# One fused attention and MoE kernel: the list of the first part in another order, and one table of engines

## The chip, the cores and the metric

One core of a Trainium2 chip runs the whole program. The metric is the device time of one execution in microseconds (us); a measurement is the median of several runs. The engines are TensorE (PE: matrix products into PSUM), VectorE (DVE), ScalarE (ACT), GpSimd (POOL) and SyncE (SP, which issues all DMAs). Each runs its own queue of instructions in order, and they wait for one another by semaphores.

## The reference

```python
def _attn_ref(q, k, v):                       # 4 batches, 8 heads, 576 positions, 64 wide
    q_d = q.reshape(B, H, Sd, 4, D).mean(axis=3)          # so do k_d and v_d; Sd = 144
    out_up = np.repeat(sm_attn(q_d, k_d, v_d), 4, axis=2)
    mask = np.abs(pos[:, None] - pos[None, :]) < 4
    scores = np.where(mask, scale * np.matmul(q, k.transpose(0, 1, 3, 2)), -1e9)
    return out_up + softmax(scores) @ v

x = attention, as 2304 tokens by 512
h = x @ w_in                                  # 512 x 2048
x = (h * (1 / (1 + np.exp(-1.702 * h)))) @ w_out           # 2048 x 512
h = x @ moe2_w_in
x = np.maximum(0.01 * h, h) @ moe2_w_out
```

## The kernel before, in words

The program has three parts that overlap. Attention works on 16 jobs, a batch and a pair of heads each, pair 0 to pair 15; four pairs make a batch and with it four rows of 128 features (kc 0 to 3) of the transposed x. The first MoE layer works on five blocks of tokens (512, 512, 512, 384, 384) by 16 slices of 128 hidden features; one such unit is 12 products for the first matrix (line 860) and 12 for the second (line 901). The second MoE layer comes last, from about 490 us.

All products are made with high parts and low parts: a number is cut into its rounded value (hi) and the rest (lo), and three products are added. So each weight tile and each block of x passes over several engines before TensorE can use it.

Up to unit 13 and attention pair 7 the order of the work is a list written out by hand, ORDER (line 52); `token` (line 1215) runs it word by word. A word is a step, a dot and a number; the part behind an @ chooses the engine (V, G or A) through `on` or `copy`, where the step asks one of these. Every engine gets its instructions in the order of this list. The words that matter here:

- `q.j`, `k.j`, `va.j`, `vb.j`, `vh.j`: loads of pair j, issued by SP. `w.n`: load of weight half n (n = 2m for the first and 2m+1 for the second matrix of slice m) into one of three buffers.
- `wF.n` (ACT, line 187), `wL.n` (DVE, 188), `wB.n` (DVE, 192): the float64 bits of a weight become float32, in one of three buffers t. `wH.n` (ACT, 159) and `wO.n` (POOL, or DVE with @V, 211): its high and low part; `wO` frees the buffer t.
- `Qd.j`, `Kd.j`: sums of four neighbours of q and k (`pool4`, line 427). It calls `nc.vector.tensor_reduce`.
- `Sd.j`, `Mxd.j`, `Exd.j`, `Rcd.j`, `Mud.j`: the attention over the sums: scores (PE, 549), row maxima (DVE, 556 and 560), exp (ACT, 566), one over the total (DVE, 519 and 520), divide (POOL, 530 and 532, or 539 from pair 4 on).
- `S0.j`, `S1.j`: local scores of one head of pairs 0 to 3 (PE, 449 and 455), into bank acc0 or acc1. `M0`, `M1` (DVE, 501) take the row maxima, `N0`, `N1` (DVE, 505) negate them, `E0`, `E1` (ACT, 510) take exp of the bank, and only then is the bank free for the next pair. `Rc.j` (519, 520) and `Mu.j` (POOL, 482) divide. Pairs 4 to 7 use `S.j` (PE, 455), `A0`, `A1` (DVE, 469), `Mx` (489), `Sb` (POOL, 482), `Ex` (ACT, 498), `Sm`, `Rc`, `Mu`.
- `T0`, `T1` (PE, 579) with `C0`, `C1` (ACT, 159) and `U0`, `U1` (PE, 651) with `D0`, `D1` transpose; `Vd.j` (PE, 632) with `Od.j` (ACT), and `Y0`, `Y1` (PE, 684) with `X0`, `X1` (DVE, 734) make the outputs, the rows of x.
- `xh.kc` (ACT, 159), `xl.kc` (843): high and low part of row kc of the first block; `h0.kc`, `h1.kc`: what units 0 and 1 make of it. `L.u`, `M.u`: the two halves of unit u; `Gt`, `Gd`, `Gh`, `Gl`: the gate between them (ACT 879, DVE 880, ACT 159, POOL or DVE 886).
- `z3.n`: n idle products in bank acc3 (line 1225), whose result nobody reads.

Behind the list a loop goes over the other units. At the end of each block it makes the high and low parts of the next one with `split_hi` and `split_lo` (line 840): there the tables XLO and (V, G, V, G) name the engine for each kc.

```python
def pool4(self, dst, src):                                       # line 426
    nc.vector.tensor_reduce(
        out=dst, in_=src.rearrange("p (g r) -> p g r", r=FACTOR), axis=AX.X, op=ALU.add
    )
XLO = [G, G, V, G]                                               # line 48
on(XLO[kc] if j < 3 else (V, G, V, G)[kc]).tensor_tensor(...)    # line 843
```

Of the kernel before, what the change touches and what calls it, by code (L numbers as in the profile page):

```python
# [7 lines left out]
F32 = mybir.dt.float32  # L8
# [5 lines left out]
ALU = mybir.AluOpType  # L14
# [13 lines left out]
def attn_moe_kernel(ctx: ExitStack, tc, qT_d, kT_d, vh_d, vg_d, w1a, w2a, w1b, w2b, outT):  # L28
# [3 lines left out]
    S = NT // B  # L32
# [14 lines left out]
    V, G = nc.vector, nc.gpsimd  # L47
    XLO = [G, G, V, G]
# [1 line left out]
    HEAD = 2  # L50
    LEAD = 3.0
    ORDER = """
        w.2 wF.2 wL.2 k.0 Kd.0 wB.2 wH.2 q.0 Qd.0 z3.14 S0.0 M0.0 S1.0 M1.0 va.4 Va0.4 Va1.4 w.0 wF.0 Sd.0 Mxd.0 Exd.0
        wO.2 wL.0 N0.0 E0.0 N1.0 Rcd.0 Mud.0 wB.0 wH.0 wO.0 k.1 q.1 z3.16 S0.1 Qd.1 Kd.1 M0.1 w.3 wF.3 wL.3 q.2 Sd.1
        Mxd.1 E1.0 Rc.0 Exd.1 vb.4 Vb0.4 wB.3 wH.3 wO.3 Vb1.4 Mu.0 Rcd.1 Mud.1 N0.1 E0.1 T0.0 C0.0 T1.0 C1.0 q.4 k.4
        z3.1 S.4 A1.4 k.2 va.1 w.1 wF.1 S1.1 M1.1 A0.4 Qd.2 Kd.2 Mx.4 Sb.4 z3.4 S0.2 M0.2 w.5 vb.7 wF.5 Qd.4 Sd.2 Mxd.2
        Exd.2 U0.0 D0.0 wL.5 N1.1 Kd.4 T0.1 k.3 z3.6 Sd.4 Rcd.2 Mud.2 wL.1 E1.1 Mxd.4 Exd.4 T1.1 C1.1 q.3 N0.2 E0.2 wB.5
        wH.5 wB.1 vb.2 Rc.1 Mu.1 Rcd.4 Mud.4 q.5 vb.0 k.5 z3.5 S.5 Qd.5 A1.5 Qd.3 A0.5 Kd.3 z3.6 U1.1 D1.1 S1.2 T0.2
        Kd.5 w.7 M1.2 wH.1 C0.1 wO.5 Vb0.7 U1.0 D1.0 wO.1 Mx.5 Sb.5 N1.2 Sd.3 S0.3 M0.3 Mxd.3 T1.4 wF.7 wL.7 va.0 T1.2
        w.4 wF.4 wL.4 w.6 wF.6 N0.3 wB.7 wB.4 E1.2 Rc.2 Mu.2 Ex.5 Exd.3 Rcd.3 Mud.3 C0.2 T0.4 C0.4 z3.4 S1.3 Vd.0 M1.3  # L60
        vh.0 Y0.0 k.6 va.6 va.5 vb.1 vh.4 C1.2 Od.0 X0.0 U0.1 D0.1 E0.3 wH.7 wO.7 C1.4 Ex.4 Y1.0 vh.1 va.2 vh.2 w.12
        vb.3 Vd.1 Od.1 w.9 X1.0 xh.0 wL.6 xl.0 N1.3 E1.3 Sm.5 wB.6 Sm.4 Rc.4 Mu.4 Rc.5 Sd.5 Mxd.5 T0.3 C0.3 Vd.4 Od.4
        wF.9 wH.4 wO.4 va.3 q.6 Vd.2 Y1.1 X1.1 h0.0 h1.0 U0.2 D0.2 T1.3 w.14 vh.3 Kd.6 Va0.5 Va1.5 Exd.5 Rc.3 C1.3 Y0.1
        U1.2 D1.2 X0.1 Qd.6 U1.4 D1.4 wL.9 Od.2 wH.6 xh.1 Y1.2 Y0.2 X1.2 Mu.3 U1.3 D1.3 U0.3 D0.3 X0.2 wF.12 xh.2 wB.9
        U0.4 D0.4 xl.1@V wO.6 xl.2 Y1.4 Vd.3 wH.9 wO.9 Od.3 Y0.3 X0.3 Y1.3 X1.3 xh.3 h0.1 wL.12 xl.3@V wF.14 wL.14 wB.12
        L.2 Gt.2 Gd.2 wH.12 wO.12@V Gh.2 Gl.2@V vb.5 Vb0.5 Rcd.5 Mud.5 w.8 wF.8 wL.8 h1.1 h1.2 h1.3 Gt.1 Gd.1 Gh.1 wB.14
        wB.8 wH.8 Gl.1@V Mu.5@V L.3 wO.8 h0.2 h0.3 Y0.4 Gt.0 Gd.0 Gh.0 X0.4 w.19 wF.19 w.15 wH.14 X1.4 Gl.0@V wL.19
        Vb1.5 L.6 wF.15 Va0.6 wL.15 wB.19 Gt.3 wO.14@V wB.15 T0.5 T1.5 C0.5 w.10 wF.10 wL.10 wH.19 wO.19 M.0 M.1 C1.5
        Vd.5 Gd.3 Gh.3 Gl.3 wB.10 wH.10 wO.10 Va1.6 Sd.6 Mxd.6 M.2 L.4 Od.5@V va.7 w.16 Gt.6 Gd.6 wF.16 wL.16 Exd.6 w.11
        wF.11 Rcd.6 Gh.6 wL.11 wB.11 wH.11 wB.16 wH.15 Gl.6@V wO.15 S.6 A0.6 A1.6 Mx.6 Mud.6 Sb.6 wO.11@V Gt.4 Gd.4  # L70
        wH.16 wO.16@V w.22 Gh.4 Gl.4@V wF.22 wL.22 vh.5 w.13 wF.13 wL.13 vb.6 w.20 wF.20 wL.20 M.3 U1.5 D1.5 U0.5 D0.5
        wB.13 wH.13 wO.13 L.5 Gt.5 wB.20 wH.20 Gd.5 Gh.5 Gl.5 Ex.6 wB.22 wH.22 wO.22 L.7 q.7 Qd.7 k.7 Kd.7 S.7 A1.7
        wO.20 Sm.6 Gt.7 Gd.7 M.4 w.18 wF.18 wL.18 wB.18 Gh.7 Gl.7@V wH.18 wO.18 Rc.6 A0.7 Mx.7 Sb.7 w.17 wF.17 wL.17 L.8
        Gt.8 Gd.8 M.5 M.6 Y0.5 t.22 w.24 X0.5 Gh.8 Gl.8@V Vb0.6 w.26 wF.26 wL.26 wB.26 Y1.5 L.9 Gt.9 wH.26 T1.6 C1.6
        w.28 wB.17 Gd.9 Gh.9 L.10 X1.5 Sd.7 Ex.7 wO.26 Mu.6@V wH.17 Gl.9@V wO.17 M.7 M.8 Sm.7 Gt.10 Gd.10 Rc.7 wF.24
        wL.24 wF.28 wL.28 wB.24 w.21 wF.21 wL.21 Mxd.7 wB.21 wB.28 wH.24 Gh.10 Gl.10@V Vb1.6 U0.6 D0.6 Exd.7 Rcd.7 Va0.7
        wH.28 L.11 Gt.11 Gd.11 T0.6 C0.6 U1.6 D1.6 Gh.11 wO.24 Mu.7@V Mud.7 wO.28@V M.9 w.23 wF.23 wL.23 wH.21 Vd.6 Od.6
        vh.6 Y1.6 w.25 wF.25 w.27 X1.6 Va1.7 Gl.11@V wB.23 wO.21@V Vb1.7 wL.25 wB.25 wF.27 wL.27 wH.23@V wO.23 L.12
        Gt.12 Gd.12 T0.7 C0.7 T1.7 L.13 t.25 wH.25 wO.25@V C1.7 w.29 w.31 Y0.6 X0.6 U0.7 D0.7 Gh.12 wF.29 wL.29 M.10
        U1.7 D1.7 Vd.7 Od.7 wB.27 wH.27 wO.27 Gl.12@V Gt.13 wF.31 Gd.13 Gh.13 Gl.13 wB.29 vh.7 Y0.7 X0.7 w.30 wF.30 Y1.7  # L80
        X1.7 wL.31 M.11 wL.30 wB.31 wH.31 wH.29 wO.29 wB.30 wH.30 wO.30 wO.31 t.27
    """
    MASKED = range(4)
    EARLY = 12
# [20 lines left out]
    def slot(name):  # L105
# [20 lines left out]
        out=ident, in_=ident, compare_op=ALU.not_equal, fill=1.0, base=0,  # L126
# [5 lines left out]
    for r in (slice(0, KT), slice(KT, P)):  # L132
        nc.gpsimd.affine_select(
            out=bands[r], in_=bands[r], compare_op=ALU.is_ge, fill=NEG, base=0,
# [3 lines left out]
            out=bands[r], in_=bands[r], compare_op=ALU.is_ge, fill=NEG, base=2 * HALO,  # L138
# [15 lines left out]
    def on(default):  # L154
        return chosen[0] or default
# [684 lines left out]
    def split_lo(j, kc):  # L840
        hi, lo = xs[kc]
        f = xf.pop((j, kc))[:, : blk[j][1]]
        on(XLO[kc] if j < 3 else (V, G, V, G)[kc]).tensor_tensor(out=lo, in0=f, in1=hi.bitcast(F32), op=ALU.subtract)  # L843

    gs = {}
    hs = {}
# [67 lines left out]
    class Second:  # L914

        B11, B12, B21, B22, T1, T2, T4 = range(7)
# [335 lines left out]
    with tc.manual_schedule(engines={ET.PE, ET.DVE, ET.Pool, ET.Activation, ET.SP}):  # L1252
# [4 lines left out]
        for kc in range(KC):  # L1257
            steps[f"xh.{kc}"] = lambda kc=kc: split_hi(0, kc)
            steps[f"xl.{kc}"] = lambda kc=kc: split_lo(0, kc)
            for m in range(HEAD):  # L1260
                steps[f"h{m}.{kc}"] = lambda kc=kc, m=m: l1_part(units[m], [kc], f"acc{m}")
# [23 lines left out]
        for u in range(UNITS, len(units)):  # L1285
            j, m = units[u]
            l1_part(units[u], range(KC))
            if m == NM - 1:
                for kc in range(KC):
                    if j + 1 < len(blk):  # L1290
                        split_hi(j + 1, kc)
                        split_lo(j + 1, kc)
# [85 lines left out]
```

## Time and profile before

| | |
|---|---|
| median of 3 runs | 851.44 us (850.66 to 851.85) |
| profiled execution | 849.98 us |
| its span | 848.2 us |
| TensorE busy | 837.6 us, 99% |
| VectorE busy | 538.5 us, 63% |
| ScalarE busy | 405.4 us, 48% |
| GpSimd busy | 474.8 us, 56% |
| chain that ended last | TensorE 94%, VectorE 2%, ScalarE, GpSimd, DMA and issue 1% each |

Times in the rows are from the start of the span. A busy share is a mean over stages that have different limits, so the stretches and the timeline are read beside it. "Idle before, releaser" at the end of a row is how long the engine had stood still, and what let it go on.

### The profile page before, as it was taken

Reading aid. Unit: us, or ns where it says so; the run is one execution under the profiler, and the core shown is the slowest. Engines: PE = TensorE matmul, PEld = TensorE weight load, DVE = VectorE, ACT = ScalarE, POOL = GpSimd, SP = SyncE. Lnnn points to the kernel's source line nnn. Section 1 sums busy time; section 2 is a strip of 40 time slices with the busy share of each in tenths; the row PEclk is TensorE's granted clock in tenths of the full one; section 3 lists DMA queues with packets and bytes.
Section 4 is the critical chain, followed back from the end, with each engine's and each line's share of the span. In section 5 each row is a group of like instructions: output and inputs, shape, how many; then the busy total and the mean of one; then the engine's idle time right before and its main releaser. Section 6 shows DMA issues by size and latency. Waiting matters only on the chain.

```text
span 848.2 us, 15692 instructions
## 1 busy us (share of the span) xinstructions
PE 837.6 (99%) x5736; PEld 761.2 (90%) x5736; DVE 538.5 (63%) x950; ACT 405.4 (48%) x972; POOL 474.8 (56%) x470
## 2 busy tenths in 40 slices
PE   8899999999999999999999999999999999999998
PEld 5677878887877888899999999999999999999997
DVE  6877776755567644567665756567564667573565
ACT  6866554433334334465555534445435464344460
POOL 6544433744446444776655823468555577454574
PEclk9999999999999999999999999999999999999999
DMA  8756545376664833999949978967779877887655
GB/s 298 248 157 183 187 145 151 111 231 180 191 198 148 243 119 123 349 346 415 364 157 338 336 252 274 345 229 275 253 263 360 275 243 261 278 290 260 217 195 177
DMA packets 76877, 204.95 MB, mean 242 GB/s; under 512 B 14656, under 2 KB 30016, under 8 KB 70400
## 3 DMA queue, kind: packets, MB, share of 16 engines
q1 hardware_dynamic: 76800, 203.95, 71.5%
q8 instruction: 45, 0.74, 0.4%
q14 instruction: 32, 0.26, 0.1%
HBM read 155.42 MB, written 48.50 MB: 240 GB/s over the span
## 4 chain that ended last, share of the span: by engine, by line
PE 94%; DVE 2%; ACT 1%; POOL 1%; DMA 1%; issue 1%; SPq 0%; POOLq 0%; ACTq 0%; DVEq 0%
PE h L860 23%; PE acc L901 23%; PE p L1107 21%; PE h L1032 21%; PE sc L455 2%; PE avd L632 1%; PE scd L549 1%; PE av L684 1%; DMA a<-qT 1%; PE av L700 0%; PE pt L651 0%; ACT a L566 0%; PE pdt L579 0%; DMA kT<-kT 0%; POOL xl L843 0%
## 5 line engine op out<-in xcount | busy, mean ns | idle before, releaser
L1086 POOL TENSOR_TENSOR ring<-raw,ring 128x384 fp32r<-128x384 f32 x148 | 166.6, 1137 | 144.6 <-ACT ring L1084 143.2
L860 PE MATMUL h<-xh,w 128*128 128x512 f32 (+1 forms) x640 | 197.6, 371 | 0.0
L1107 PE MATMUL p<-ring,v 128*128 128x384 f32 x900 | 178.8, 334 | 0.0
L901 PE MATMUL acc<-gh,w 128*128 128x512 f32 (+1 forms) x560 | 173.5, 372 | 0.0
L1107 PEld LDWEIGHTS p<-ring,v 128*128 128x128 f32 x900 | 158.0, 188 | 0.1
L1032 PE MATMUL h<-x,v 128*128 128x384 f32 x672 | 137.3, 334 | 0.0
L860 PEld LDWEIGHTS h<-xh,w 128*128 128x128 f32 x640 | 118.7, 188 | 16.8 <-issue 1.2
L886 POOL TENSOR_TENSOR gl<-g,gh 128x512 fp32r<-128x512 f32 (+1 forms) x59 | 72.2, 1224 | 96.8 <-ACT gh L159 96.2
L1032 PEld LDWEIGHTS h<-x,v 128*128 128x128 f32 x672 | 118.3, 188 | 0.0
L860 PE MATMUL h<-xl,w 128*128 128x512 f32 (+1 forms) x320 | 117.8, 368 | 0.4 <-POOL xl L843 0.4
L901 PEld LDWEIGHTS acc<-gh,w 128*128 128x128 f32 x560 | 104.0, 188 | 15.1 <-issue 0.6
L901 PE MATMUL acc<-gl,w 128*128 128x512 f32 (+1 forms) x280 | 103.7, 370 | 0.0
L880 DVE SCALAR_TENSOR_TENSOR g<-g,h 128x512 f32<-128x512 f32 (+1 forms) x80 | 50.4, 630 | 76.5 <-ACT g L879 76.2
L879 ACT ACTIVATE g<-h 128x512 f32<-128x512 f32 (+1 forms) x80 | 43.9, 549 | 98.5 <-PE h L860 96.6
L1039 ACT ACTIVATE raw<-raw 128x384 f32<-128x384 f32 x72 | 37.9, 526 | 108.9 <-DVE raw L1042 108.7
L1072 DVE TENSOR_TENSOR raw<-raw,raw 128x384 f32<-128x384 f32 x84 | 76.7, 947 | 15.1 <-ACT raw L1039 13.0
L1042 DVE TENSOR_TENSOR raw<-h,u 128x384 f32<-128x384 f32 x72 | 40.1, 557 | 72.1 <-PE h L1032 71.6
L1084 ACT ACTIVATE ring<-raw 128x384 fp32r<-128x384 f32 x150 | 73.5, 515 | 0.0
L1032 PE MATMUL h<-x_ra,v 128*128 128x384 f32 x336 | 72.5, 334 | 0.0
L159 ACT ACTIVATE gh<-g 128x512 fp32r<-128x512 f32 (+1 forms) x70 | 41.7, 595 | 63.5 <-DVE g L880 59.6
L860 PEld LDWEIGHTS h<-xl,w 128*128 128x128 f32 x320 | 60.1, 188 | 7.8 <-POOL xl L843 0.9
L211 POOL TENSOR_TENSOR w<-t,w 128x512 fp32r<-128x512 f32 x25 | 33.1, 1328 | 49.0 <-ACT w L159 42.9
(188 smaller groups left out, 1268.2 us busy)
## 6 DMA issues: line engine op xcount, KB each, us to landing
v<-ws SPq DMA_DIRECT2D x42, 1024.0 KB, 6.2
v<-ws SPq DMA_DIRECT2D x72, 512.0 KB, 4.9
ws<-wo SPq DMA_DIRECT2D x16, 1792.0 KB, 10.3
s<-w1a SPq DMA_DIRECT2D x16, 512.0 KB, 4.4
s<-w2a SPq DMA_DIRECT2D x16, 512.0 KB, 4.5
s<-w1b SPq DMA_DIRECT2D x16, 512.0 KB, 5.8
s<-w2b SPq DMA_DIRECT2D x16, 512.0 KB, 9.8
v<-ws SPq DMA_DIRECT2D x24, 256.0 KB, 4.3
```

Of the source, the lines that this page charges most:

```text
L159: return nc.scalar.activation(out=out, in_=in_, func=AF.Copy, scale=scale)
L860: nc.tensor.matmul(h, w[:, kc * P : (kc + 1) * P], xs[kc][part], start=kc == 0 and i == 0, stop=kc == KC - 1 and i == 2,)
L879: lambda: nc.scalar.activation(out=g, in_=h[:, :n], func=AF.Tanh, scale=0.5 * 1.702),
L880: lambda: nc.vector.scalar_tensor_tensor(out=g, in0=g, scalar=1.0, in1=h[:, :n], op0=ALU.add, op1=ALU.mult),
L886: lambda: on(G).tensor_tensor(out=gl, in0=g, in1=gh.bitcast(F32), op=ALU.subtract),
L901: nc.tensor.matmul(acc[c][:, :n], w[:, cs], g, start=m == 0 and i == 0, stop=m == NM - 1 and i == 2)
L1032: nc.tensor.matmul(h, w[:, a, ks], x, start=not more and kt == 0 and k == 0, stop=kt == 1 and k == 2, skip_group_check=True,)
L1042: nc.vector.tensor_tensor(out=out, in0=h, in1=u, op=ALU.add)
L1072: nc.vector.tensor_tensor(out=o, in0=a, in1=b, op=ALU.subtract)
L1084: nc.scalar.activation(out=hi, in_=t, func=AF.Copy)
L1086: e.tensor_tensor(out=lo, in0=t, in1=hi.bitcast(F32), op=ALU.subtract)
L1107: nc.tensor.matmul(self.bank[pair, ct][:, :N2], w[:, q, a, cs], g, start=not more and q == 0 and k == 0, stop=q == QC - 1 and k == 2, skip ...
```

## The change

Two edits. The first replaces the list ORDER. It has the same 599 words but for the idle products (z3.16 and one z3.6 became z3.13 and one z3.5: 52 in all, not 56), in another order, and with other engines at 28 of them: `Kd.1` to `Kd.5` and `Qd.3` carry @G; `C0.3`, `C1.3`, `C1.4`, `C1.6`, `Vb1.5`, `wO.6`, `wO.8`, `wO.9` and others carry @V now, and `Gl.2`, `Gl.4`, `Gl.6`, `Gl.7`, `Gl.9`, `Gl.11` no longer do. The second is one number in `split_lo`: the third block (j = 2) now takes the row V, G, V, G.

```diff
     ORDER = """
-        w.2 wF.2 wL.2 k.0 Kd.0 wB.2 wH.2 q.0 Qd.0 z3.14 S0.0 M0.0 S1.0 M1.0 va.4 Va0.4 Va1.4 w.0 wF.0 Sd.0 Mxd.0 Exd.0
-        wO.2 wL.0 N0.0 E0.0 N1.0 Rcd.0 Mud.0 wB.0 wH.0 wO.0 k.1 q.1 z3.16 S0.1 Qd.1 Kd.1 M0.1 w.3 wF.3 wL.3 q.2 Sd.1
-        Mxd.1 E1.0 Rc.0 Exd.1 vb.4 Vb0.4 wB.3 wH.3 wO.3 Vb1.4 Mu.0 Rcd.1 Mud.1 N0.1 E0.1 T0.0 C0.0 T1.0 C1.0 q.4 k.4
...
-        Kd.5 w.7 M1.2 wH.1 C0.1 wO.5 Vb0.7 U1.0 D1.0 wO.1 Mx.5 Sb.5 N1.2 Sd.3 S0.3 M0.3 Mxd.3 T1.4 wF.7 wL.7 va.0 T1.2
-        w.4 wF.4 wL.4 w.6 wF.6 N0.3 wB.7 wB.4 E1.2 Rc.2 Mu.2 Ex.5 Exd.3 Rcd.3 Mud.3 C0.2 T0.4 C0.4 z3.4 S1.3 Vd.0 M1.3
...
+        k.0 Kd.0 q.0 w.2 wF.2 Qd.0 z3.14 wL.2 va.4 wB.2 S0.0 M0.0 S1.0 M1.0 N0.0 Va0.4 Va1.4 Sd.0 wH.2 w.0 wF.0 wO.2
+        Mxd.0 wL.0 Exd.0 N1.0 E0.0 E1.0 k.1 z3.13 wB.0 Rcd.0 q.1 S0.1 Qd.1 Mud.0 wH.0 Kd.1@G Sd.1 w.3 M0.1 wO.0 Mxd.1
+        wF.3 q.2 Rc.0 wL.3 wB.3 Exd.1 T0.0 vb.4 T1.0 C0.0 k.4 wH.3 Mu.0 Rcd.1 Mud.1 Vb0.4 q.4 N0.1 E0.1 S.4 Qd.4 C1.0
...
+        A0.5 U1.1 T0.2 D1.1 U1.0 D1.0 wO.5 M1.2 wO.1 Kd.5@G T1.4 Mx.5 S0.3 w.4 N1.2 wF.4 Sb.5 wF.7 E1.2 Sd.3 Mxd.3 w.6
+        z3.4 Rc.2 M0.3 Exd.3 vb.1 Ex.5 wL.7 N0.3 Rcd.3 S1.3 C0.2 va.0 T1.2 wF.6 Qd.5 Mud.3 wB.7 T0.4 C0.4 vh.0 wL.4 Mu.2
...
     def split_lo(j, kc):
         hi, lo = xs[kc]
         f = xf.pop((j, kc))[:, : blk[j][1]]
-        on(XLO[kc] if j < 3 else (V, G, V, G)[kc]).tensor_tensor(out=lo, in0=f, in1=hi.bitcast(F32), op=ALU.subtract)
+        on(XLO[kc] if j < 2 else (V, G, V, G)[kc]).tensor_tensor(out=lo, in0=f, in1=hi.bitcast(F32), op=ALU.subtract)
```

Three places of the order follow, where the prediction speaks of them. First VectorE, from the sums of pair 2 to the second weight of pair 2's stretch (a_2_0 holds q and k of pair 2, kd_0 the sums of k of pair 4, scd the banks of Sd, stat_1 what N1.1 writes). Before:

```order
L427 TENSOR_REDUCE a_2_0_301<-a_2_0_301 128x144 x2
L489 TENSOR_REDUCE stat_0_7_218<-P_0_4_215 128x10
L501 TENSOR_REDUCE sc_2_10_413<-sc_2_10_413 128x5
L427 TENSOR_REDUCE qd_0_1_212<-q_0_11_354 128x144
L556 TENSOR_REDUCE scd_2_11_442<-scd_2_11_442 128x3
L560 TENSOR_SCALAR stat_d_2_7_305<-scd_2_11_442 128x3
L188 TENSOR_SCALAR s_2_1_426<-s_2_1_426 128x512
L505 TENSOR_SCALAR stat_1_6_260<-sc_1_13_390 128x5
L427 TENSOR_REDUCE kd_0_2_213<-kT_0_12_356 128x144
L519 TENSOR_SCALAR stat_d_2_7_305<-stat_d_2_7_305 128x3
```

And after the change:

```order
L427 TENSOR_REDUCE a_2_0_311<-a_2_0_311 128x144 x2
L501 TENSOR_REDUCE sc_1_12_380<-sc_1_12_380 128x5
L501 TENSOR_REDUCE sc_2_11_405<-sc_2_11_405 128x5
L489 TENSOR_REDUCE stat_0_7_190<-P_0_4_187 128x10
L556 TENSOR_REDUCE scd_2_12_426<-scd_2_12_426 128x3
L560 TENSOR_SCALAR stat_d_2_7_315<-scd_2_12_426 128x3
L427 TENSOR_REDUCE kd_0_2_185<-kT_0_11_335 128x144
L188 TENSOR_SCALAR s_2_1_433<-s_2_1_433 128x512
L519 TENSOR_SCALAR stat_d_2_7_315<-stat_d_2_7_315 128x3
L520 RECIPROCAL stat_d_2_7_315<-stat_d_2_7_315 128x3
L505 TENSOR_SCALAR stat_1_6_258<-sc_1_12_380 128x5
```

`Kd.2@G` (in the x2) and `Kd.4@G` (kd_0) are on VectorE as before, Kd.4 one step earlier; N1.1 (L505) moved from ahead of Rcd.2 (L519, L520) to behind it.

Second, GpSimd in the same stretch (a_0_1 and a_1_1 are what Mu.0 and Mu.1 divide, a_1_2 and a_2_2 what Mud.1 and Mud.2 do, pd_0 Mud.4, P_0_4 Sb.4; w with t_1_1 is wO.3, with t_2_1 wO.5). Before:

```order
L211 TENSOR_TENSOR w_0_227<-t_0_0_226,w_0_227 128x512
L440 TENSOR_TENSOR vg_0_10_326<-vg_0_10_326 48x2x128
L211 TENSOR_TENSOR w_1_157<-t_1_1_298,w_1_157 128x512
L440 TENSOR_TENSOR vd_0_3_214<-vg_0_10_326 48x128
L482 TENSOR_TENSOR a_0_1_161<-a_0_1_161,stat_0_6_163 128x640
L530 TENSOR_TENSOR a_1_2_259<-a_1_2_259,stat_d_1_7_261 128x3x128
L532 TENSOR_TENSOR a_1_2_259<-a_1_2_259,stat_d_1_7_261 128x3x64
L482 TENSOR_TENSOR P_0_4_215<-P_0_4_215,stat_0_7_218 128x640
L530 TENSOR_TENSOR a_2_2_303<-a_2_2_303,stat_d_2_7_305 128x3x128
L532 TENSOR_TENSOR a_2_2_303<-a_2_2_303,stat_d_2_7_305 128x3x64
L482 TENSOR_TENSOR a_1_1_258<-a_1_1_258,stat_1_6_260 128x640
L539 TENSOR_TENSOR pd_0_6_217<-pd_0_6_217,stat_d_0_8_219 128x432
```

After:

```order
L482 TENSOR_TENSOR a_0_1_155<-a_0_1_155,stat_0_6_157 128x640
L530 TENSOR_TENSOR a_1_2_257<-a_1_2_257,stat_d_1_7_259 128x3x128
L532 TENSOR_TENSOR a_1_2_257<-a_1_2_257,stat_d_1_7_259 128x3x64
L440 TENSOR_TENSOR vg_0_10_328<-vg_0_10_328 48x2x128
L440 TENSOR_TENSOR vd_0_3_186<-vg_0_10_328 48x128
L530 TENSOR_TENSOR a_2_2_313<-a_2_2_313,stat_d_2_7_315 128x3x128
L532 TENSOR_TENSOR a_2_2_313<-a_2_2_313,stat_d_2_7_315 128x3x64
L211 TENSOR_TENSOR w_1_165<-t_1_1_309,w_1_165 128x512
L482 TENSOR_TENSOR a_1_1_256<-a_1_1_256,stat_1_6_258 128x640
L539 TENSOR_TENSOR pd_0_6_189<-pd_0_6_189,stat_d_0_8_191 128x432
L482 TENSOR_TENSOR P_0_4_187<-P_0_4_187,stat_0_7_190 128x640
L211 TENSOR_TENSOR w_2_439<-t_2_1_438,w_2_439 128x512
```

Mu.0 moved up to stand right behind wO.0 (w_0, not shown after), wO.3 moved down behind Mud.2, and Sb.4 behind Mud.4.

Third, ScalarE at pair 0 (a_0_1 with sc_0_10 is E0.0, with sc_0_11 E1.0; w_0 is wH.0, t_1_1 wF.3, a_1_2 Exd.1). Before:

```order
L566 ACTIVATE a_0_2_162,stat_d_0_7_164<-scd_0_12_229,stat_d_0_7_164 128x144 x3
L510 ACTIVATE a_0_1_161,stat_0_6_163<-sc_0_10_186,stat_0_6_163 128x64 x5
L159 ACTIVATE w_0_227<-t_0_0_226 128x512
L187 ACTIVATE t_1_1_298<-s_1_1_296 128x512
L510 ACTIVATE a_0_1_161,stat_0_6_163<-sc_0_11_199,stat_0_6_163 128x64 x5
L566 ACTIVATE a_1_2_259,stat_d_1_7_261<-scd_1_11_307,stat_d_1_7_261 128x144 x3
```

After:

```order
L566 ACTIVATE a_0_2_156,stat_d_0_7_158<-scd_0_12_224,stat_d_0_7_158 128x144 x3
L510 ACTIVATE a_0_1_155,stat_0_6_157<-sc_0_10_195,stat_0_6_157 128x64 x5
L510 ACTIVATE a_0_1_155,stat_0_6_157<-sc_0_11_208,stat_0_6_157 128x64 x5
L159 ACTIVATE w_0_235<-t_0_0_234 128x512
L187 ACTIVATE t_1_1_309<-s_1_1_303 128x512
L566 ACTIVATE a_1_2_257,stat_d_1_7_259<-scd_1_11_296,stat_d_1_7_259 128x144 x3
```

E1.0 moved ahead of wH.0 and wF.3.

## Rows read from the trace of the kernel before

**Rows 1.** Stretches: us, engines' busy time, PEclk, DMA share, GB/s.

```profile
45.20:56.80 11.60, 9.98 (x168) 8.03 (x165) 8.36 (x18) 8.13 (x24) 7.34 (x7) 1.00 0.44 125
57.00:255.00 198.00, 198.00 (x1578) 158.75 (x1578) 132.34 (x270) 91.18 (x202) 92.06 (x101) 1.00 0.58 175
255.00:262.00 7.00, 6.57 (x29) 5.09 (x29) 5.07 (x8) 4.23 (x12) 6.02 (x6) 1.00 0.09 30
262.00:840.00 578.00, 577.98 (x3409) 558.64 (x3407) 354.50 (x564) 266.91 (x590) 341.60 (x317) 1.00 0.77 268
```

**Rows 2.** Chain that ended last: start us, us, what.

```profile
1.65 4.62 DMA a<-qT
...
11.05 1.49 ACT a L510 x10
...
28.50 1.40 PE idle L1225 x6
...
33.53 1.10 PE pdt L579 x9
...
257.37 3.00 POOL xl L843 x2
```

**Rows 3.** Timeline of TensorE, first products: start us, us, engine, line, instruction.

```profile
0.99 4.84 PE L1225 MATMUL idle<-warm 128*128 128x512 bf16 x14 [0.99 <-POOL warm L119]
```

**Rows 4.** Timeline, two places where VectorE and GpSimd overlap.

```profile
43.46 1.27 POOL L843 TENSOR_TENSOR xl<-xf,xh 128x512 fp32r<-128x512 f32 x1 [0.29 <-ACT xh L159]
43.57 1.19 DVE L519 TENSOR_SCALAR stat<-stat 128x10 f32<-128x10 f32 x1
...
373.83 0.69 DVE L192 SCALAR_TENSOR_TENSOR s<-b,s 128x512 uint32<-128x512 uint32 x1
...
374.10 1.02 POOL L886 TENSOR_TENSOR g4l<-g,g4h 128x384 fp32r<-128x384 f32 x1 [0.82 <-ACT g4h L159]
374.44 0.97 DVE L188 TENSOR_SCALAR s<-s 128x512 uint32<-128x512 uint32 x1
```

**Rows 5.** Timeline: wO.0, wB.3, N0.1, Mu.0 and Mud.4.

```profile
13.16 1.27 POOL L211 TENSOR_TENSOR w<-t,w 128x512 fp32r<-128x512 f32 x1
...
15.69 0.63 DVE L192 SCALAR_TENSOR_TENSOR t<-t,s 128x512 uint32<-128x512 uint32 x1
...
17.06 0.14 DVE L505 TENSOR_SCALAR stat<-sc 128x5 f32<-128x5 f32 x1
...
18.96 1.25 POOL L482 TENSOR_TENSOR a<-a,stat 128x640 f32<-128x640 f32 x1
...
28.53 0.91 POOL L539 TENSOR_TENSOR pd<-pd,stat_d 128x432 f32<-128x432 f32 x1
```

**Rows 6.** Timeline: Rcd.4, N1.2, E1.2, S1.3, Vd.0, h0.0.

```profile
27.09 0.11 DVE L519 TENSOR_SCALAR stat_d<-stat_d 128x3 f32<-128x3 f32 x1
...
32.45 0.16 DVE L505 TENSOR_SCALAR stat<-sc 128x5 f32<-128x5 f32 x1
...
33.85 0.30 ACT L510 ACTIVATE a<-sc,stat 128x64 f32<-128x64 f32 x1
...
35.48 0.30 PE L449 MATMUL sc<-bands_b,ident_b 128*128 128x320 bf16 x1
...
36.43 1.47 PE L632 MATMUL avd<-a,a 128*64 128x144 f32 x18
...
45.21 0.50 PE L860 MATMUL h<-xh,w 128*128 128x512 f32 x1
```

**Rows 7.** Timeline of ScalarE: wF.9, and what it waited for.

```profile
46.99 0.68 ACT L187 ACTIVATE t<-s 128x512 f32<-128x512 f32 x1 [1.61 <-DMA s<-w2a]
```

**Rows 8.** Timeline: Gl.0, and the first product that reads it.

```profile
68.79 1.52 DVE L886 TENSOR_TENSOR gl<-g,gh 128x512 fp32r<-128x512 f32 x1
...
71.10 0.39 PE L901 MATMUL acc<-gl,w 128*128 128x512 f32 x1
```

**Rows 9.** TensorE's waits, the longest kind: us in total, times, longest us.

```profile
PE sc L455 <- DMA kT<-kT: 1.3, 1, 1.3
```

## What the change should do to the time

> **What bounds the kernel.** I read the table by stretches first [rows 1]. From 57 us on, TensorE is busy in every microsecond: 198.00 of 198 up to 255, 577.98 of 578 from 262 to 840. The one hole is 0.43 us between 255 and 262. So all that comes after 57 us has a fixed length, and the change can move the time in three places only: the moment at which TensorE gets into that unbroken stretch, the hole at 257 us, and any new hole. Then I read the chain that ended last [rows 2]: before 57 us it changes engine at every step, the usual sign of a list in which five engines wait for one another in turn. At 257 us it names two low parts of GpSimd (L843, 3.00 us for two) as what TensorE waits for. For the stretch before 57 us I then went along the timeline of each engine and marked where each step stands.
>
> **What the order of instructions says.** `Kd.1` to `Kd.5` carry @G in the list, but pool4 (L427) calls VectorE whatever is chosen, and the order shows all of them on VectorE. So the sums of k do not move. The rest of the list is nevertheless arranged as if VectorE had those five sums less to do, and GpSimd five pieces more. That is where I look for the loss.
>
> **The port.** One thing decides how VectorE and GpSimd fit together [rows 4]. A VectorE step on 128x10 numbers (L519) took 1.19 us at 43.57, while GpSimd worked on a low part from 43.46 to 44.73; alone it takes 0.17 or less (0.11 at 27.09, [rows 6]). At 373.83 an L192 runs, GpSimd's next step is in its queue at 374.10, and the L188 that VectorE starts at 374.44 takes 0.97: GpSimd, which asked first, had its turn between the two. So L188, L192, L519 and a low part on VectorE take turns with GpSimd, instruction by instruction, while L427 (reductions) does not. The Trainium skill, SBUF — State Buffer, "Who interferes with whom", says that the two share a pair of ports under an exclusive lock, and that "Issue order, not op shape, decides who blocks"; these rows agree. By that rule alone GpSimd would also never delay a reduction, so that the sums of k could stay on VectorE at no cost to GpSimd; that leaves my sum as it is.
>
> **The sum, in order of time** (against the profiled execution, 849.98 us with a span of 848.2; the median of the runs is 851.44, and I add the difference to that).
>
> 1. Head. Before, the first scores waited for q until 1.65 + 4.62 = 6.27 [rows 2]; k and q are now loaded ahead of w.2, and the 14 idle products end at 0.99 + 4.84 = 5.83 [rows 3]. The gain is between 0 and 0.44; I take 0.4, since VectorE now has w.2's two steps ahead of the first row maxima.
> 2. `E1.0` stands right behind `E0.0` on ScalarE. E0.0 then ends at 12.1 (12.54 less 0.4), E1.0 at 13.6 (1.49 more), and wO.0, which began 0.62 behind E0.0 (13.16), begins at 14.2 and holds the port until 15.5 [rows 2, 5]. Rc.0 (L519) waits for that, and Mu.0, moved up from 18.96, is ready at once: it takes its 1.25 us ahead of wB.3. wB.3 goes from 15.69 to about 17.1 and N0.1 from 17.06 to about 18.1: 1.0 later [rows 5]. If GpSimd let VectorE go first it would be 0.
> 3. N1.1 now stands behind Rcd.2, which waits for Exd.2, and the four idle products (0.23 each, [rows 2]) now lie between S0.2 and Sd.2, on the path. E1.1 comes about 1.2 later.
> 4. On GpSimd Mud.2 is moved ahead of wO.3, and Sb.4 behind Mud.4. It waits for Rcd.2 until about 25.3, with wO.3 idle behind it, where before the queue had been emptied. After that wO.3 (1.27) and Mu.1 (1.25) take the port in turn with wB.5, wB.1 and the two L519: Rcd.4, at 27.09 before, comes at about 30.5. Qd.5 moves out from behind it (0.7 back) and a wait of some 0.5 goes, so N1.2 moves from 32.45 to about 34.9 [rows 6].
> 5. wF.7 needs the buffer that wO.1 frees. wO.1 is behind Mud.4, Sb.4 and wO.5 on GpSimd: 0.91 + 1.25 + 1.27 + 1.27 = 4.7 us from 30.9 [rows 5, 6], so 35.6. E1.2 stands behind wF.7 (0.68, as in [rows 7]): 36.2, not 33.85. S1.3 needs the bank that E1.2 frees: 37.8, not 35.48, 2.35 later [rows 6].
> 6. T1.2 and T0.4, ahead of S1.3 before, are behind it: six products, 1.10 x 6/9 = 0.73 [rows 2]. Vd.0 goes from 36.43 to about 39.4, and h0.0 from 45.21 to about 48.2: 3.0 later [rows 6].
> 7. From there TensorE had 11.60 - 9.98 = 1.62 us of holes up to 56.8 [rows 1]. ScalarE stood 1.61 us waiting for w.9 with wH.4 behind it [rows 7]; in the new list wH.4 goes first and w.9 is loaded ahead of w.12. As TensorE arrives later and this queue is no longer held, I take 1.5 of the 1.62 back. Y1.4 only moves behind h0.1. Entry: 3.0 - 1.5 = 1.5 later. The ends are 3.0 (nothing back) and -1.4 (below).
> 8. Low parts of the third block. kc 0 goes to VectorE, so kc 1 is the first on GpSimd and could be ready 1.5 us earlier (3.00/2, [rows 2]): gain up to the whole 0.43. But two on each side share the port and go in turn, and both divides (L482) of GpSimd lie ahead. I take 0.2, ends 0 and 0.43.
> 9. Gl.0. Before, it ended at 68.79 + 1.52 = 70.31 and the first product that reads it began at 71.10 [rows 8]: 0.8 us to spare. Now X0.4, wB.14, Vb1.5 and wL.19 stand between: some 1.6 us of VectorE more. I take 0.2 for a hole there, ends 0 and 1.2.
> 10. Four idle products fewer (0.9 us) count nothing by themselves: TensorE waits there instead. w.4's load now waits for wB.1 and holds up va.0 and vh.0 in SP's queue; they should land just ahead of Vd.0, hidden by step 5, and cost up to 1 us if step 5 does not happen.
>
> Sum: +1.5 - 0.2 + 0.2 = +1.5, so 852.9 us. 0.2% is 1.7 us, about what a measurement of this kernel can tell from no change; the forecast is a small loss that lies just inside that.
>
> **Rivals.**
> A second answer to steps 2, 4 and 5 (**the delays are absorbed**): VectorE gets the port first, or GpSimd has drained earlier than I think, and E1.2 starts where it did, or 0.4 sooner. Then Vd.0 is 0.73 - 0.4 = 0.3 later, and 1.3 to 1.6 of the holes in step 7 still goes: -1.0 to -1.3, with step 8 about -1.4, 850.0 us. For it: TensorE is the busiest engine from Vd.0 on, and step 7's gain comes from the order alone. Against: rows 4.
>
> **The clock falls.** By the steps above TensorE stands nearly idle from 17.6 to 20.0 and from 35.2 to 37.8, longer than any wait of before (1.3 us, [rows 9]). Before, the granted clock was 1.00 in every stretch [rows 1], with those shorter waits; that speaks against it, but does not reach so far. The first 14 idle products of the program took 0.35 us each, and 0.23 later [rows 2, 3], so TensorE is slower after having stood still. At 1.2 GHz, S0.2, the four idle products and Sd.2 (about 2.5 us) would take up to twice as long on the path: +2.5 on top, 855.4 us. It decides if either hole is as long as I say. The Trainium skill, TensorE: Matmul & The Clock Gate, "What's actually happening", says that the array's clock is halved when it has been idle; the first products agree, and by that page this case would be the likelier one.
>
> **A late part stops the steady stretch**: Gl.0 at the bound of step 9, or vh.0 late: +1.1 on the forecast, 854.0 us.
>
> **The sums do run on GpSimd**: VectorE would have five times 0.7 us less and steps 3 to 5 would shrink. The order excludes it; no chance is kept for it.
>
> **How the numbers follow.** My forecast 0.60 (spread +-1.3: 0.34 within 0.2%, 0.26 slower), absorbed 0.18 (0.08 faster, 0.10 within), the clock 0.15 (slower), a late part 0.07 (0.04 slower, 0.03 within). Together faster 0.08, within 0.47, slower 0.45. The range goes from 850.2, which leaves out half of the absorbed case, to 855.8, which takes in the clock: 0.84 of the chance or so. The forecast's own range is 851.6 to 854.2.
>
> **What would show it.** Right: L427 five times on VectorE; wB.3 ending with Mu.0's end near 17.2; GpSimd standing from 20.7 to 25; E1.2 on ScalarE past 35.5; h0.0 past 47; a hole at 257 us of under 0.43. Wrong: E1.2 at or before 33.85, or h0.0 at or before 45.2 (then the absorbed case); a granted clock under 1.00 before 57 us (the clock); a hole of TensorE between 57 and 160 us (a late part).

## The result, and the profile after

The changed kernel takes 857.4 us (median of 6 executions, 854.37 to 858.71), the kernel before 851.04 beside it: ratio 1.0067, interval 1.0046 to 1.0087. That is a loss of 6.4 us by the medians and of 5.7 by the ratio. I had forecast a small loss (852.9, 1.5 us) in a range up to 855.8; the loss is four times as large and lies outside. The medians here and below are over all executions, while the ratios leave out one slow execution of head_new (1652 us).

First the table of stretches, now also for 10 to 28 us (us, engines' busy time, PEclk, DMA share, GB/s; the rows from 10 to 28 us show TensorE alone). The kernel before:

```profile
10.00:14.00 4.00, 3.88 (x41) 1.00 1.03 358
14.00:18.00 4.00, 4.00 (x80) 1.00 1.04 327
18.00:21.00 3.00, 2.30 (x37) 1.00 0.89 268
21.00:28.00 7.00, 4.81 (x53) 1.00 0.58 166
```

The changed kernel:

```profile
10.00:14.00 4.00, 1.88 (x18) 1.00 1.03 339
14.00:18.00 4.00, 4.00 (x72) 0.58 1.05 360
18.00:21.00 3.00, 1.96 (x41) 0.99 0.86 220
21.00:28.00 7.00, 6.87 (x44) 0.53 0.31 96
...
45.20:56.80 11.60, 10.91 (x160) 8.28 (x158) 11.42 (x30) 9.17 (x39) 8.65 (x8) 1.00 0.76 246
57.00:255.00 198.00, 194.30 (x1572) 154.91 (x1571) 146.19 (x269) 90.64 (x200) 90.02 (x93) 1.00 0.55 164
255.00:262.00 7.00, 7.00 (x81) 5.61 (x81) 2.14 (x4) 2.67 (x6) 4.33 (x7) 1.00 0.88 257
262.00:840.00 578.00, 577.98 (x3401) 556.93 (x3397) 358.41 (x573) 271.61 (x605) 341.77 (x317) 1.00 0.77 266
```

Three things differ from [rows 1]. TensorE stands 2.12 us between 10 and 14, and after that its granted clock is 0.58 from 14 to 18 and 0.53 from 21 to 28: for most of these stretches it ran at 1.2 instead of 2.4 GHz. Between 57 and 255, where it never stood still before, it now stands 3.70 us. And the hole at 257 us is gone. The timeline of the changed kernel shows where (rows picked from the views of several engines: start us, us, engine, line, instruction, in brackets the idle time before and its releaser):

```profile
8.36 2.98 PE L1225 MATMUL idle<-warm 128*128 128x512 bf16 x13
13.46 0.30 PE L449 MATMUL sc<-bands_b,ident_b 128*128 128x320 bf16 x1 [2.12 <-ACT a L510]
...
14.31 1.33 PE L549 MATMUL scd<-a 64*64 64x144 f32 x11
...
17.11 1.32 POOL L482 TENSOR_TENSOR a<-a,stat 128x640 f32<-128x640 f32 x1 [0.36 <-DVE stat L520]
17.42 1.55 DVE L192 SCALAR_TENSOR_TENSOR t<-t,s 128x512 uint32<-128x512 uint32 x1
...
18.68 0.80 PE L455 MATMUL sc<-a 64*64 64x64 f32 x20
20.52 0.52 PE L651 MATMUL pt<-ident,a 128*128 128x128 f32 x3 [1.04 <-DVE P L469]
21.17 0.30 PE L449 MATMUL sc<-bands_b,ident_b 128*128 128x320 bf16 x1
21.39 1.30 PE L455 MATMUL sc<-a 64*64 64x64 f32 x20
...
39.99 0.30 PE L449 MATMUL sc<-bands_b,ident_b 128*128 128x320 bf16 x1 [0.26 <-ACT a L510]
...
41.72 1.47 PE L632 MATMUL avd<-a,a 128*64 128x144 f32 x18
...
51.01 0.50 PE L860 MATMUL h<-xh,w 128*128 128x512 f32 x1
...
88.31 1.43 POOL L886 TENSOR_TENSOR gl<-g,gh 128x512 fp32r<-128x512 f32 x1 [5.49 <-ACT gh L159]
88.52 1.25 DVE L519 TENSOR_SCALAR stat_d<-stat_d 128x3 f32<-128x3 f32 x1
...
90.75 0.50 PE L901 MATMUL acc<-gl,w 128*128 128x512 f32 x1 [1.14 <-DVE gl L886]
...
95.16 0.33 SPq L168 DMA_DIRECT2D s<-w2a  x1
...
98.79 0.43 DVE L188 TENSOR_SCALAR s<-s 128x512 uint32<-128x512 uint32 x1 [3.03 <-DMA s<-w2a]
...
113.86 0.50 PE L860 MATMUL h<-xh,w 128*128 128x512 f32 x1 [2.07 <-DVE w L211]
```

- The 13 idle products end at 11.34, and S0.1 waits for E0.0 until 13.46. Twenty products of L455 that take 0.80 at 18.68, with the clock up, take 1.30 at 21.39.
- wB.3 (17.42) takes 1.55 for 0.63 before [rows 5], while Mu.0 runs on GpSimd from 17.11 to 18.43.
- S1.3, Vd.0 and h0.0 come at 39.99, 41.72 and 51.01; before 35.48, 36.43 and 45.21 [rows 6].
- M.3 waits 1.14 for Gl.3: Rcd.6 (L519), ahead of it on VectorE, took 1.25, while Gl.6 ran on GpSimd.
- The load of w.13 is issued only at 95.16, VectorE stands 3.03 us for it (ScalarE 3.69), and at unit 9 TensorE waits 2.07 us for the low part wO.18.

### The profile page after: what moved, and what is told of

Read it like the earlier page. It is cut to its first block, busy times and chain, and to the rows that moved or that the text cites. A ratio compares the mean times of both kernels' runs of the same rounds, so it can differ in the third digit from the quotient of the medians.

```text
span 856.1 us, 15672 instructions
## 1 busy us (share of the span) xinstructions
PE 842.4 (98%) x5732; PEld 762.6 (89%) x5732; DVE 558.4 (65%) x959; ACT 404.6 (47%) x968; POOL 475.6 (56%) x465
## 4 chain that ended last, share of the span: by engine, by line
PE 86%; DVE 9%; DMA 2%; ACT 2%; issue 1%; SPq 0%; DVEq 0%; ACTq 0%
PE p L1107 21%; PE h L1032 20%; PE acc L901 20%; PE h L860 20%; DVE t L192 2%; DMA s<-w1a 1%; PE scd L549 1%; DMA s<-w2a 1%; PE avd L632 1%; DVE s L188 1%; PE sc L455 1%; DVE w L211 1%; PE av L684 1%; ACT a L510 1%; DVE stat L489 1%
## 5 line engine op out<-in xcount | busy, mean ns | idle before, releaser
L886 POOL TENSOR_TENSOR gl<-g,gh 128x512 fp32r<-128x512 f32 (+1 forms) x63 | 78.6, 1248 | 121.6 <-ACT gh L159 117.7
L901 PEld LDWEIGHTS acc<-gl,w 128*128 128x128 f32 x280 | 52.6, 188 | 8.3 <-DVE gl L886 1.5
```

Of the source, the lines that this page charges most:

```text
L886: lambda: on(G).tensor_tensor(out=gl, in0=g, in1=gh.bitcast(F32), op=ALU.subtract),
L901: nc.tensor.matmul(acc[c][:, :n], w[:, cs], g, start=m == 0 and i == 0, stop=m == NM - 1 and i == 2)
```

## The experiments

Each was run beside the kernel before, with 4 to 11 executions. Where the list is a line longer, its line numbers are one higher (L450 for L449). The times, in the order in which they were run:

| run | median us | before, beside it | ratio (interval) |
|---|---|---|---|
| low_only | 849.57 | 850.32 | 0.9991 (0.9983 to 1.0000) |
| head_new | 853.33 | 850.32 | 1.0031 (1.0020 to 1.0043) |
| tail_new | 854.02 | 850.32 | 1.0048 (1.0033 to 1.0063) |
| fill | 856.56 | 850.32 | 1.0078 (1.0061 to 1.0094) |
| w2_first | 856.92 | 850.47 | 1.0074 (1.0062 to 1.0086) |
| engines_before | 860.12 | 850.47 | 1.0112 (1.0099 to 1.0125) |
| fill_two | 856.02 | 850.47 | 1.0062 (1.0049 to 1.0075) |
| queue_back | 856.26 | 850.47 | 1.0069 (1.0053 to 1.0084) |
| w13_early | 854.90 | 850.38 | 1.0048 (1.0036 to 1.0060) |
| head_back | 855.84 | 850.38 | 1.0051 (1.0032 to 1.0070) |
| mended | 851.33 | 850.38 | 1.0012 (1.0003 to 1.0020) |
| low_w9 | 849.49 | 850.38 | 0.9989 (0.9981 to 0.9998) |
| before_less | 852.08 | 850.54 | 1.0012 (1.0002 to 1.0021) |
| w13_fill | 852.31 | 850.54 | 1.0025 (1.0013 to 1.0037) |
| mended_fill | 849.93 | 850.54 | 0.9993 (0.9983 to 1.0002) |

### low_only: the second edit alone

```diff
-        on(XLO[kc] if j < 3 else (V, G, V, G)[kc]).tensor_tensor(out=lo, in0=f, in1=hi.bitcast(F32), op=ALU.subtract)
+        on(XLO[kc] if j < 2 else (V, G, V, G)[kc]).tensor_tensor(out=lo, in0=f, in1=hi.bitcast(F32), op=ALU.subtract)
```

> The kernel before with the second edit alone (third block's low parts two and two). The trace of the changed kernel shows no hole of TensorE at the border of the third block, where the kernel before had 0.43 us. If that comes from the edit: the hole is gone here too, and the time is 0.4 us under the kernel before. If my step 8 was right: about 0.2 us of hole is left. If the hole only went because TensorE came there 8 us later: it stays 0.43 and the time does not change.

The stretch around the border of the third block (TensorE):

```profile
255.00:262.00 7.00, 7.00 (x32) 1.00 0.24 68
```

The hole is gone, in the old order. TensorE got to the border 0.85 us later in this profile than in that of the kernel before, but a late arrival is not the cause: before_less (below) keeps the old table, gets there 3.2 us later, and waits the same 0.43 us ahead of 263.58. So the edit does it, and takes away the whole 0.43 us; the medians differ by 0.75, with an interval that ends at no change.

### head_new and tail_new: half of each list

```diff
+ head_new: ORDER = the new list up to L.2, then the words that are left as in the list before
+ tail_new: ORDER = the list before up to L.2, then the words that are left as in the new list
```

> The new list up to L.2 (62 us), from there the words that are left in the order and with the engines of the list before. Theory A (two separate losses: the clock in the first 30 us, and VectorE overloaded with low parts and G steps from 85 to 114 us): the granted clock falls as in the changed kernel (under 0.9 somewhere from 12 to 28 us), TensorE's holes from 62 to 160 us fall from 3.6 us to under 1, time 3 to 5 us over the kernel before. Theory B (all of the loss arises before 57 us, the later holes are only its echo): holes after 62 us stay near 3.6 us and the time is that of the changed kernel, 6 us over.

> The list before up to L.2, from there the words that are left in the order and with the engines of the new list. Theory A: granted clock 1.00 as in the kernel before; TensorE's holes from 62 to 160 us stay near 3.6 us; time 2.5 to 3.5 us over the kernel before (third block's gain of 0.4 taken off). Theory B: holes after 62 us go to under 0.5 and the time is within 0.5 us of the kernel before.

Stretches of head_new (TensorE):

```profile
14.00:30.00 16.00, 14.35 (x160) 0.79 0.63 202
...
62.00:160.00 98.00, 98.00 (x712) 1.00 0.52 163
```

Stretches of tail_new (TensorE):

```profile
14.00:30.00 16.00, 13.28 (x204) 1.00 0.81 242
...
70.00:100.00 30.00, 29.50 (x218) 1.00 0.60 186
100.00:160.00 60.00, 57.34 (x409) 0.97 0.48 149
```

The first half loses 3.0 us with a fallen clock and without a late hole, the second 3.7 with 3.2 us of late holes and the clock up before them. Of theory A it holds that there are two losses, and that the later one is no echo of the earlier; what makes the later one is asked below. (In tail_new the granted clock also fell behind the late hole: 0.97.)

### fill, fill_two, w2_first: is it the clock, or the load of w.2?

```diff
- ... z3.13 wB.0 ...  S1.1 U0.0 A1.4 ...
+ ... z3.22 wB.0 ...  S1.1 z3.4 U0.0 A1.4 ...    # fill;  fill_two has z3.11 for z3.4
- k.0 Kd.0 q.0 w.2 wF.2 ...
+ w.2 k.0 Kd.0 q.0 wF.2 ...                      # w2_first
```

> The changed kernel with 13 idle products more: z3.13 ahead of S0.1 is z3.22 (9 x 0.23 = 2.07 us against the hole of 2.12), and z3.4 stands ahead of U0.0 (4 x 0.23 = 0.9 against the hole of 1.04). They delay nothing that is ready. Clock theory: the granted clock stays 1.00 up to 57 us, S1.3 comes at 37 to 38 and not 39.99, and the time is 3 to 5 us under the changed kernel (852.5 to 854.5). Queue theory (the steps were late by the order of VectorE and GpSimd, and the clock fell in time that was waiting anyway): the clock stays 1.00, but S1.3 still comes after 39 and the time is within 1 us of the changed kernel.

> The changed kernel with z3.22 ahead of S0.1 and z3.11 ahead of U0.0. In the run with z3.22 and z3.4 a hole of 1.60 us was left ahead of U0.0 and the granted clock still fell for one piece behind it (0.89 from 14 to 30 us). Clock theory: with both holes covered the granted clock is 1.00 before 57 us in most executions, S1.3 comes 1 to 2 us before 39.58, and the median is 1.5 to 3 us under the changed kernel (854.4 to 856). Queue theory: clock 1.00, but S1.3 still after 39 and the median within 1 us of the changed kernel. In both, the share of what is left is the order's own.

> The changed kernel with w.2 as the first word again, so that its load is issued ahead of k.0 and q.0. In the changed kernel w.2's data came at 7.60 us and VectorE stood with its first weight step ahead of the first row maxima, so that E0.0 went from 11.81 to 13.32 where it was 10.94 to 12.44 before (my step 1 had it 0.4 earlier, not 0.9 later). If the load is the cause: wL.2 at 4.5 to 5.5 and E0.0's end at 12.0 to 12.5, TensorE's hole ahead of S0.1 falls from 2.12 to 1.0 to 1.3 us, and, if nothing behind takes the gain back, the time is 0.9 to 1.3 us under the changed kernel, more where the granted clock now stays at 1.00. If the first row maxima were late for another reason: E0.0's end stays at 13.2 to 13.4.

`fill` covered the first hole only; 1.60 us stayed ahead of U0.0, the clock fell behind it in the profiled execution (mean 0.89 from 14 to 30), S1.3 came at 39.58, and the median did not move clear of the changed kernel's. `fill_two` covered both (TensorE):

```profile
14.00:30.00 16.00, 14.84 (x219) 1.00 0.75 230
...
100.00:160.00 60.00, 57.73 (x410) 0.97 0.48 154
```

The clock stays up before 57 us, S1.3 comes at 37.62 and Vd.0 at 39.35: 2.4 us earlier than in the changed kernel. But behind the late hole the clock falls instead (0.97), so that the time (ratio 1.0062) gains little: 5.55 us over the kernel before, where the changed kernel was 6.4 over. `w2_first` refutes the load of w.2: E0.0 began at 11.70 with it (11.81 without), since on VectorE wL.2 and wB.2 stand behind Qd.0 and ahead of the row maxima, and so wait for q either way. (The hole ahead of S0.1 did shrink to 0.78, but because the idle products began later, at 9.59 and not 8.36; a hole of 2.58 then stood ahead of U0.0.) The list before gave 11.51 in low_only and 10.94 in the profile of before, so most of what separates the two lists there is a difference between executions.

### engines_before: is it VectorE's extra work?

```diff
- wO.15@V  wO.18@V  wO.20@V  Gl.3@V  Gl.4  Gl.6  Gl.7  ...
+ wO.15    wO.18    wO.20    Gl.3    Gl.4@V  Gl.6@V  Gl.7@V  ...   # all engines of the list before
```

> The changed kernel in its new order, with the engines of the list before at all of the words that changed engine (low parts 6, 8, 9, 15, 18, 20 and others back to GpSimd, Gl.2, Gl.4, Gl.6, Gl.7 and others back to VectorE). Theory E (VectorE is overloaded from 85 to 114 us by the engines' choice): TensorE's holes from 62 to 160 us go from 3.6 to under 1 us, time 2.5 to 3.5 us under the changed kernel. Theory O (the order of the words makes the holes, such as w.13 and w.20 converted 10 to 14 us later): holes stay over 2 us and the time is within 1.5 us of the changed kernel.

(The engines of 31 words differ between the lists, not of 28.) Theory O holds in that the holes stay, but the time does not: the new order with the old engines is the slowest of all. TensorE's stretch and its late waits:

```profile
100.00:160.00 60.00, 56.18 (x402) 0.97 0.48 146
...
108.84 0.51 PE L580 MATMUL pdt<-ident,pd 128*48 128x128 f32 x3 [1.12 <-POOL pd L540]
...
114.48 0.50 PE L861 MATMUL h<-xh,w 128*128 128x512 f32 x1 [2.38 <-POOL w L212]
```

Unit 9 waits 2.38 us for the same low part wO.18, now on GpSimd. The order of the words makes the late holes with either set of engines: from 70 to 160 they add up to 3.82 us here and to 1.14 + 2.42 = 3.56 in the changed kernel. Why this run is still 3.3 us slower than the changed kernel is not settled; the clock fell behind the late hole (0.97), which it did not in the changed kernel's profile, and TensorE waits 1.35 us ahead of 53.31.

### w13_early: one place in the queue of loads

```diff
- ... D1.5 w.26 q.7 ... wB.20 w.13 Sb.6 ... L.8 w.28 ...
+ ... D1.5 w.13 q.7 ... wB.20 Sb.6 ... L.8 w.26 w.28 ...
```

> The changed kernel with the load of w.13 where it has that of w.26, and w.26 where it is needed, ahead of w.28. In the new list w.26 takes the third of the three load buffers 12 words ahead of w.13, so w.13's load waits until wB.20 is done (95.09) and lands at 98.70; VectorE stands 3.03 us and ScalarE 3.69 us for it, and what they have to convert then is late at unit 9 (hole of 2.07 us at 111.8). Theory buffer (that one place in the load queue makes the late hole, neither the engines' choice nor the entry): VectorE's and ScalarE's wait goes to under 1 us, TensorE's holes from 100 to 160 us from 2.4 to under 0.5 us, time 2 to 4 us under the changed kernel (853.4 to 855.4). Theory load on VectorE (28 steps of other engines): the wait for w.13 goes, but over 1.2 us of hole stays, time within 1.2 us of the changed kernel.

Stretches (TensorE):

```profile
14.00:30.00 16.00, 14.77 (x169) 0.79 0.67 196
...
70.00:100.00 30.00, 29.29 (x237) 1.00 0.65 192
100.00:160.00 60.00, 59.67 (x427) 1.00 0.49 155
```

The load of w.13 goes out at 87.67, VectorE's and ScalarE's waits for it are gone, and of 2.42 us of holes from 100 to 160 remain 0.33. Theory buffer holds. The clock still falls early. The median is 4.5 us over the kernel before, where the changed kernel was 6.4 over: 1.9 us for the place of these two loads, just under what was expected. The intervals of the two ratios overlap, so this difference alone is not clear of noise; w13_fill below gives a clearer pair.

### queue_back and head_back: the words of my steps 2 to 4

```diff
+ queue_back: E1.0 behind wF.3, wO.3 behind wH.3, Sb.4 behind Mx.4, N1.1 behind M1.1
+ head_back:  the same, and U0.0, D0.0 behind Exd.2
```

> The changed kernel with four words moved back to where the list before has them: E1.0 behind wF.3, wO.3 behind wH.3, Sb.4 behind Mx.4, N1.1 behind M1.1 (my steps 2, 3 and 4). If my steps were right: wB.3 about 1 us earlier (from 17.42 to 16.4), E1.1 two us or more earlier (28.79 to 26.8 or less), Rcd.4 3 us earlier or more (32.81 to under 30), S1.3 from 39.99 to under 38, time 1.5 to 3 us under the changed kernel. Rival (the clock and the head's late load set these times, the words' places do not): E1.1 and Rcd.4 move by under 1 us, time within 0.7 us of the changed kernel.

> The changed kernel with the four words of the run queue_back moved back, and U0.0 and D0.0 behind Exd.2 as in the list before. In queue_back E0.1 came 1.4 us earlier (18.17 for 19.54), but U0.0, which the new list has ahead of S0.2, then held TensorE 2.94 us for Mu.0, and the granted clock fell behind that hole. If these words make the head's loss: S0.2 at 19.5 to 20.2 (21.17 in the changed kernel), no hole over 1.3 us from 14 to 30 us and the granted clock 1.00 there in most executions, Vd.0 at 38 to 39 (41.72), time 2.5 to 4.5 us under the changed kernel. If the head's loss lies in other words (the order of loads, Rcd.4's queue): S0.2 moves, but Vd.0 stays over 40 and the time falls by under 1.5 us.

Both moved wB.3 to about 16.5 and E0.1 to 18.2 or earlier (over 1.3 us earlier for E0.1), as step 2 has it, and both gained little, for TensorE met another hole. S1.3 came at 39.26 in queue_back, not under 38. In queue_back U0.0 waits for Mu.0:

```profile
20.91 0.90 PE L652 MATMUL pt<-ident,a 128*128 128x128 f32 x3 [2.94 <-POOL a L483]
```

In head_back, with U0.0 out of the way, S0.2 is early (19.36) but has nothing ahead of it:

```profile
19.36 0.30 PE L450 MATMUL sc<-bands_b,ident_b 128*128 128x320 bf16 x1 [1.86 <-ACT a L511]
19.59 1.28 PE L456 MATMUL sc<-a 64*64 64x64 f32 x20
```

The new list has z3.4 behind S0.2, where the list before has it ahead. The clock fell in both runs, against the expectation; Vd.0 moved from 41.72 to 38.32 in head_back, but the late hole stayed.

### mended and mended_fill

```diff
+ mended:      head_back and w13_early together, z3.16 ahead of S0.1
+ mended_fill: the same, and z3.8 ahead of S0.2
```

> The two runs beside this together, with z3.16 in place of z3.13 ahead of S0.1. If the head and w.13 are the whole loss: 850.5 to 852.5, within 0.2% of the kernel before, granted clock 1.00 up to 160 us in most executions. If something else of the new list still costs (Gl.0, the hole at 90 us of 1.1 us, entry late by the queue of ScalarE): 853 to 855.

> The kernel mended with eight idle products more, ahead of S0.2, where it had a hole of 1.86 us and the granted clock fell for two pieces from 19.8 to 26.7. Clock theory: clock 1.00 in most executions and 849.3 to 850.5, 1 to 2 us under mended (851.33). If the clock is not what is left: 851 to 851.7, as mended.

From 14 to 30 us (TensorE), first mended, then mended_fill:

```profile
14.00:30.00 16.00, 14.14 (x160) 0.79 0.70 220
```

```profile
14.00:30.00 16.00, 15.11 (x221) 1.00 0.79 236
```

Eight words moved and three idle products more take the new list from 6.4 us over the kernel before to 0.95 over; eight idle products more, ahead of S0.2, take it to 0.6 under, an interval that includes no change. Little else of the new list costs anything (the gain of the second edit, 0.43 us or more, is in this figure).

### before_less and w13_fill: the clock alone, and the order alone

```diff
- ... k.1 q.1 z3.16 S0.1 ...          # kernel before
+ ... k.1 q.1 z3.7 S0.1 ...           # before_less
+ w13_fill: the edits of w13_early and of fill_two together
```

> The kernel before with z3.7 in place of z3.16 ahead of S0.1, nothing else: nine idle products (2.07 us) fewer, so that TensorE stands about 2.1 us where it had no hole. Nothing else waits for them. Clock theory: the granted clock falls to 0.50 for one piece or two somewhere from 13 to 28 us in most executions, the time is 1 to 3 us over the kernel before. If a hole of that length does not bring the clock down by itself: granted clock 1.00 in this stretch, time within 0.5 us of the kernel before.

> The changed kernel with w.13's load ahead of w.26's (the late hole is gone) and with z3.22 ahead of S0.1 and z3.11 ahead of U0.0 (the two early holes are covered): what is left is the order's own cost with the clock up. w13_early gave 854.9. Clock theory: clock 1.00 in most executions, Vd.0 at 39.0 to 39.8, time 852.2 to 853.4, which is what my steps 1 to 6 gave without their clock. If the clock was paid out of time that was waiting anyway: 854.4 to 855.2.

The timeline of before_less:

```profile
9.53 1.69 PE L1226 MATMUL idle<-warm 128*128 128x512 bf16 x7
13.28 0.30 PE L450 MATMUL sc<-bands_b,ident_b 128*128 128x320 bf16 x1 [2.06 <-ACT a L511]
13.50 0.80 PE L456 MATMUL sc<-a 64*64 64x64 f32 x20
14.21 1.64 PE L550 MATMUL scd<-a 64*64 64x144 f32 x12
```

The same products in the kernel before:

```profile
13.51 0.95 PE L549 MATMUL scd<-a 64*64 64x144 f32 x12
```

A hole of 2.06 us, with nothing else changed, brings the clock down (mean 0.89 from 14 to 30): the twelve products of Sd.1 take 1.64, where they took 0.95. It costs 1.5 us by the medians, 1.0 by the ratio (1.0012, interval 1.0002 to 1.0021). That is one fall of the clock by itself; in the profile of the changed kernel it fell twice. w13_fill is the other half: new order, clock up, no late hole. Its stretches and its timeline:

```profile
14.00:30.00 16.00, 14.74 (x216) 1.00 0.77 231
...
100.00:160.00 60.00, 59.70 (x434) 1.00 0.47 147
```

```profile
37.73 0.30 PE L450 MATMUL sc<-bands_b,ident_b 128*128 128x320 bf16 x1 [0.26 <-ACT a L511]
...
39.46 1.47 PE L633 MATMUL avd<-a,a 128*64 128x144 f32 x18
...
48.70 0.50 PE L861 MATMUL h<-xh,w 128*128 128x512 f32 x1
```

It takes 852.31, 1.8 us over the kernel before (ratio 1.0025). So the loss of 6.4 us divides, by medians each against the kernel before beside it: 6.4 - 4.5 = 1.9 for the late hole, 4.5 - 1.8 = 2.7 for the clock, 1.8 for the order of the head with the gain of the second edit in it. By the ratios the three are 1.6, 2.0 and 2.1.

This split holds for one order of taking away. Taken away the other way round, the clock first, it reads: 6.36 - 5.55 = 0.8 for the clock (fill_two), 5.55 - 1.77 = 3.8 for the late hole (fill_two against w13_fill, whose intervals lie apart). The reason is in the profiles: with the early holes covered, the clock falls behind the late hole instead. So the two together cost 4.6 us, more than taking away either alone gives back: 0.8 (not clear of noise) and 1.9.

### low_w9: my step 7 alone, in the kernel before

```diff
- ... vh.2 w.12 vb.3 Vd.1 Od.1 w.9 X1.0 ... wF.9 wH.4 wO.4 ... Exd.5 Rc.3 ...
+ ... vh.2 w.9 w.12 vb.3 Vd.1 Od.1 X1.0 ... wH.4 wO.4 ... Exd.5 wF.9 Rc.3 ...   # with the second edit
```

> The kernel before with the second edit, and with my step 7 alone: w.9's load ahead of w.12's, and wF.9 behind Exd.5 instead of ahead of wH.4. In the kernel before ScalarE stood 1.61 us for w.9 with wH.4 and D0.2 behind it, and TensorE had 1.62 us of holes from 45.2 to 56.8. If step 7 was right: these holes go to under 0.5 us, entry 1.0 to 1.5 us earlier, time 848 to 848.8 (low_only gave 849.57). If the holes have other causes (Exd.5's row maxima, Mu.3): they stay over 1.2 us and the time is within 0.4 us of low_only.

ScalarE's wait for w.9 is gone, and TensorE's holes are not: 11.60 - 10.58 = 1.02 us from 45.2 to 56.8, where low_only had 1.13. 849.49 against 849.57 is no difference. TensorE's longest wait there is now 0.69 us, for ScalarE's copy (L160) ahead of 50.94; that the wait for w.9 was one of several which end at nearly the same time fits this, but no run separates them. This version has the lowest median of all and beats the kernel before with an interval clear of no change (0.9981 to 0.9998); that it is faster than low_only is not shown.

## Why the prediction was wrong

Steps 1 to 6, the order of the head, with the start that I gave for each and the two that were measured:

| | forecast | changed kernel | w13_fill (clock up) |
|---|---|---|---|
| wB.3 | 17.1 | 17.42 | 17.42 |
| N0.1 | 18.1 | 19.18 | 19.19 |
| E1.1 | 25.3 | 28.80 | 26.69 |
| E1.2 | 36.2 | 38.38 | 36.10 |
| S1.3 | 37.8 | 39.99 | 37.73 |
| Vd.0 | 39.4 | 41.72 | 39.46 |
| h0.0 | 48.2 | 51.01 | 48.70 |

With the clock up the steps hold to within 0.1 us from E1.2 to Vd.0, though partly by errors that cancel (E1.1 came 1.4 later than I said, what follows it took less). Step 1's gain did not come: E0.0 ended at 13.32, not 12.1, as wL.2 and wB.2 stand ahead of the first row maxima; I had named them and still booked a gain. That it became a loss is not shown: E0.0 began between 10.94 and 11.97 in the five profiles with the old head, and between 11.21 and 12.19 in those with the new one. The forecast of a loss of 1.5 us is close to what the order alone costs, 1.8 in w13_fill, but that is partly luck: h0.0 came 0.5 later than forecast and step 7 gave back less.

Four things failed.

1. **Step 10: "Four idle products fewer (0.9 us) count nothing by themselves: TensorE waits there instead."** This is the step that failed: a wait of TensorE was priced at nothing. Behind the hole of 2.12 us ahead of S0.1 the granted clock fell to 0.58, and before_less shows such a fall with no other change. The three idle products missing there are 0.7 us of that hole. Another 0.5 is the gain of step 1 itself, as the first scores were done earlier and the idle products began at 8.36, not 8.84; the rest is E0.0, which ended later. The second fall, from about 21.5 on (0.53), came behind the 1.04 us ahead of U0.0, a wait that no step had. fill_two, which covered both holes, kept the clock at 1.00.
2. **The clock as a rival of 0.15.** Its price was about right (2.5 us forecast, 2.7 by the medians of w13_early and w13_fill, 2.0 by their ratios), its chance was not, and I put it beside the forecast as an alternative, though the order's delays and the clock's fall add up. I looked for long holes at 17.6 to 20.0 and 35.2 to 37.8; the longest came at 11.3, where I had priced the missing products at nothing. The Trainium skill, TensorE: Matmul & The Clock Gate, "What's actually happening", has the clock halve after idleness; the granted clock of 0.58 and 0.53 behind the holes agrees. That holes of the length I forecast would be enough was my reading and does not stand on the page.
3. **"A late part stops the steady stretch"**, chance 0.07, at Gl.0 or vh.0, 1.1 us. The case came, but elsewhere and larger. Gl.0 made no hole. Gl.3 made one of 1.14, by the taking of turns at the port that I had described [rows 4]; and w.13, loaded behind w.26, made one of 2.07. I worked the list out step by step only up to h0.1, and apart from Gl.0 took the steady stretch behind it as given, though the words had moved there too. That the word w.26 takes one of three buffers ahead of w.13 and is converted only behind unit 8 (at 111 us), stands in the list and could have been read there.
4. **Step 7: "I take 1.5 of the 1.62 back."** Counted over the 11.8 us from h0.0 on, 0.55 us of holes are left in the changed kernel and 0.92 in w13_fill, where the kernel before had 1.62: 1.1 and 0.7 came back. But low_only, in the old list, has 1.13 left as well, and low_w9, with step 7 alone, 1.02. So most of what came back is not shown to be due to step 7.

Right were: the sums of k stay on VectorE (L427 on it throughout), the turns with GpSimd at the port as the cause of wB.3's delay, GpSimd standing idle for Rcd.2, and step 8 in its direction (0.2 forecast, 0.43 measured). In the sum, the terms 1.5 - 0.2 + 0.2 should have read, by the medians: order of the head about 2.2, low parts -0.4, clock 2.7, late hole 1.9 (clock and late hole together 4.6). Both signs that I had named for these two cases, a granted clock under 1.00 before 57 us and a hole between 57 and 160 us, came.

## What to carry to other kernels

An idle product that nobody reads is not free to take away: a hole in front of a chain costs its length only if something waits for it, but it can cost the clock behind it. When a list of steps is ordered anew, go through the whole list, and for every load ask which buffer it takes and until when: a load issued early for a late use takes a buffer from the one that is needed next. And cases that do not exclude each other can come together: their costs belong in one sum, and are not to be weighed against each other.

## What was not expected of the hardware

- Executions of one and the same kernel differ by the clock that was granted. The changed kernel took 854.4 and 854.5 us in two executions with a mean granted clock of 0.998, 857.3 and 857.5 in two at 0.996, 857.9 and 858.7 in two at 0.994.
- Length alone does not say whether the clock falls. Behind holes of 1.04 (changed kernel, ahead of U0.0), 1.60, 1.86, 2.06, 2.12, 2.58 and 2.94 us it fell in the profiles above (2.58 in w2_first); behind 1.38 ahead of S0.1 in mended_fill, 1.59 at 28 us in low_only and 1.82 at 30 us in before_less it did not. Behind the late hole of 2.07 us it fell in head_back (0.97 from 100 to 160) and not in the changed kernel (1.00). What decides is left open.
- The hole itself differs between profiles: ahead of S0.1, with the same 13 idle products, it was 2.12 us in the changed kernel, 2.11 in w13_early and 1.77 in head_new, but 0.92 in queue_back and 0.87 in head_back, where the idle products began later (9.59 and 9.17, not 8.36) and the clock stayed up there.
- Order and engines cannot be judged apart. With the engines of the list before, the new order took 860.12 us, 9.6 over the kernel before beside it; with its own it was 6.4 over. The old order with the new engines was not run.
